# Four token tables, no arithmetic on GpSimd, a new plan: an attention, FFN and MoE kernel in FP32

## The chip, the cores and the metric

The kernel runs on one core of a Trainium2 chip. Time is the device time of one execution, in microseconds, the median of several runs. Engines: PE (TensorE), DVE (VectorE), ACT (ScalarE), POOL (GpSimd) and SP (SyncE, here a DMA queue). Each engine works through its own instructions in order.

## The reference

```python
# attention: B=4, H=12, S=448, D=64, cap=30
scores = cap * tanh(scale * q @ k.T / cap)
attn = softmax(scores)
x = (attn @ v), heads side by side       # 1792 tokens x 768
# feed-forward 768 -> 2048 -> 768
h = x @ w_in
x = (h * sigmoid(1.702 * h)) @ w_out
# top-1 mixture of 8 experts, 768 -> 1024 -> 768
e = argmax(x @ w_gate)
out = prob[e] * sigmoid(x @ w_output_gate)[e] * (relu(x @ w1[e]) @ w2[e])
```

All in FP32.

## The kernel before

**Products.** An FP32 product is made of three passes on numbers in a shorter FP32 form (fp32r): each operand is split into a high part (a cast, `rnd_any`, on ACT, DVE or POOL, lines 361, 476 and 480) and a rest (a subtraction, `rest_any`, line 484, on DVE or POOL). The passes are hi x hi, hi x lo and lo x hi. The splits of weights and of activations are most of what DVE, ACT and POOL do.

**Order.** A planner written in Python (`Plan`, from line 112) holds every piece of work as a task: its engine or a choice of engines with a cost each (`c_rnd`, `c_rest`, line 495 on), its dependencies, the buffers that it takes, a latency after it, and a due value. The due value is a place in a schedule (constants such as `W1`, `F3`, `SLOT`) less a lead by the kind of task (the table `LEAD`). The planner simulates the engines and emits each engine's instructions in the order that comes out; on the chip an engine then keeps that order, and waits for semaphores where its operands are not ready.

**Stages.** Attention runs batch by batch; per pair of heads POOL's queue carries three small transfers of the normalisation (`s_ld` L697, `s_st` L705, `r_ld` L709). The FFN runs in halves per batch (matmuls `fps`, lines 970 to 972; activation `th`, lines 990 and 994), interleaved with the attention of the batches that follow. After a batch's second half, `route` (from line 1069) works out its routing:

- `lp`, small DVE steps, and a one-hot matrix `ohb`; the matmuls `cps` (L1093 to 1096) count how many tokens of each expert come before each token;
- DVE adds the running counts `carry` and gets a position per token, `posi` (L1126 to 1130), and then the new `carry` (L1133);
- four indirect DMAs on POOL's queue (L1099), one per 112 tokens, write the token numbers to these positions of a table `tab` in DRAM. All four write the same tensor;
- the factor (probability x output gate) is written as column 768 of each token's row, and the rows go to DRAM (`x2s`).

So `route` runs four times, once per batch. After it the MoE runs in slots of 128 tokens of one expert: 20 that always run and one in a branch. The first three (`NEARLY`) take their tokens from the first three batches, the others from the counts of all four. `enumerate_tiles` (L1216 to 1238) and the three steps ahead of it (L1523 to 1525) turn the counts into slots, in some 25 small DVE steps. `token_ids` gathers the slots' rows of `tab` (POOL, `tg`, L1262), PE transposes them (`ptg`, L1269), and DVE makes token indices `gi` and output indices `si` (L1274, L1275). Per slot: gather the tokens (`xg`, POOL, L1360, ring of 3), transposes `xtp` (L1373), 36 matmuls `hps` (L1403), relu, transposes `gtp` (L1421), 48 matmuls `ops` (L1453), ACT's output scaled by column 768 of `xg` (`out_y`, L1460), and an indirect DMA to the output (POOL, L1463). A slot splits 14 chunks of weights, 6 of 1024 and 8 of 768 columns, from loads `w1r` and `w2r` into a ring of 4 (`w`) and one of 5 (`mw`) buffers.

The FFN's weights are split once, stored in DRAM (`wsp`) and loaded again (`w<-wsp`) for later batches.

Of the kernel before, what the change touches and what calls it, by code (L numbers as in the profile page):

```python
# [9 lines left out]
F32 = mybir.dt.float32  # L10
# [11 lines left out]
DM = H * D  # L22
# [19 lines left out]
LEAD = {'tanh': -0.33, 'v_hi': 0.96, 'pv2': -9.09, 'tr': 3.33, 'x2_cp': -17.4, 'relu': 1.05, 'th': 11.2, 'g_hi': 21.35, 'x2_hi': 0.71, 'x2_lo': -6.7, 'transp': 7.51, 'w_s': -0.38, 'cap_max': -2.34, 'v_lo': -4.0, 'mms': 4.58, 'x2_tr': 0.76, 'pv_x': -11.56, 'scores': 5.25, 'q_hi': -25.2, 'lo': -6.51, 'ld_qk': 12.09, 'o_acc': 2.27, 'g_lo': -9.62, 'k_hi': 5.63, 'exp': -1.51, 'p_hi': 2.76, 'eps': -23.42, 'quantum': -2.12, 'w_e': 5.66, 'st_': 3.4, 'hi': 2.08, 'gmul': -4.78, 'pv1': -8.53, 'pv_add': 1.74, 'pv_cp': 18.5, 'p_lo': 5.55, 'logit': -5.59, 'norm': -0.71, 'x_hi': 5.44, 'out_y': 2.93, 'o_x2': 5.14, 'w_1': 2.98, 'w_2': 5.49, 'x_lo': 5.68, 'recip': -20.85, 'ld': -8.2, 'ld_v': 1.8, 'k_lo': 3.19, 'q_lo': 3.16, 'u_cp': 0.0, 's_ld': 1.21, 's_rc': -0.1, 's_st': 0.07, 'r_ld': -10.16, 'f': 18.48, 'v_f': 5.49}  # L42
TICK = 10.24 / 3
WFR = 2
W1 = 117.952
W2 = 199.014
W3 = 220.117
AF1 = 0.797
AF2 = 0.777
AF3 = 0.741  # L50
AO1 = -13.626
AO2 = 7.441
AO3 = 18.073
# [8 lines left out]
ATT0 = 2.681  # L62
HID = 0
F3 = 163.508
# [9 lines left out]
SLAT = (2.8, 4.6, 5.8)
VPL = 6.822
STG = -1.173
GL = 30.335
XIN = 9.159
HL = 10.771
XAL = 41.739  # L80
SPLIT = True
CV0 = 132.598
CV1 = 66.827
MWB = 5
SLOT = 17.742
# [28 lines left out]
class Plan:  # L114
# [6 lines left out]
        ("DVE", "PE"): 0.2, ("DVE", "ACT"): 0.13, ("DVE", "DVE"): 0.13, ("DVE", "POOL"): 0.2,  # L121
# [219 lines left out]
def tile_softcap_attention_ffn_moe(  # L341
# [38 lines left out]
    tab = dram.tile([NE * ECAP, 1], F32, name="tab")  # L380
# [67 lines left out]
    def program(ctx, general):  # L448
# [82 lines left out]
        def attention(b):  # L531
# [14 lines left out]
            for h in range(H):  # L546
# [59 lines left out]
                if qkf:  # L606
                    t_q = t_k = t_qk
                else:
                    x = add({"ACT": (c_act(S, 0.19), 0.0), "POOL": (0.62, POOLD, True), "DVE": (0.36, HID, True)}, q_hi, vp, [t_qk], [qkr, qks])
# [223 lines left out]
        def single(u, c, vw):  # L833
# [32 lines left out]
            x2 = add({"POOL": (0.00083 * m + 0.16, 0.0, True), "DVE": (0.00052 * m + 0.07, HID, True)}, w_s, vw, [x], [rb, gb])  # L866
# [199 lines left out]
        routed = {}  # L1066

        def route(b, lx, lb, tcp, tokb, vq):
# [5 lines left out]
            def chain(x, eng, uses, ops):  # L1074
                for c, f in ops:
                    x = add(one(eng, c), lambda e, f=f: f(), vq, [x], uses)
                return x
# [26 lines left out]
            def lg(n):  # L1104
# [6 lines left out]
            xlt = chain(x, "DVE", [rb, tb1], [(0.13, lambda: nc.vector.tensor_copy(tl("lt", [CK, NC4, 16]), R["lp"]))])  # L1111
            xls = chain(xlt, "DVE", [rb], [
                (0.1, lambda: red(out=tl("m", [CK, NC4, 1]), in_=lg("lt"), axis=AX.X, op=ALU.max)),
                (0.1, lambda: vt(out=tl("ls", sh), in0=lg("lt"), in1=bc(R["m"], sh), op=ALU.subtract)),
            ])
            xoh = chain(xls, "DVE", [rb], [
                (0.1, lambda: vt(out=tl("eq", sh), in0=lg("lt"), in1=bc(R["m"], sh), op=ALU.is_equal)),
                (0.1, lambda: vt(out=R["eq"], in0=R["eq"], in1=bc(pr, sh), op=ALU.mult)),
                (0.1, lambda: red(out=tl("mx", [CK, NC4, 1]), in_=R["eq"], axis=AX.X, op=ALU.max)),
                (0.1, lambda: vt(out=tl("oh", sh), in0=R["eq"], in1=bc(R["mx"], sh), op=ALU.is_equal)),  # L1120
            ])
            x = chain(xoh, "DVE", [rb], [(0.1, lambda: nc.vector.tensor_copy(tl("ohb", sh, BF16), R["oh"]))])
# [475 lines left out]
```

## Time and profile before

| | before |
|---|---|
| median of 3 runs | 1177.28 us (1174.28 to 1177.40) |
| the profiled execution | 1172.92 us |
| its span | 1171.1 us |
| PE, DVE, ACT, POOL busy | 94%, 77%, 68%, 28% of the span |

The span is the stretch between the first and the last recorded instruction. Busy times are unions per engine; a matmul's end is modelled. A row of a time line gives start, duration, engine, line, operation and operands, and in brackets how long the engine stood before it and what ended that. PEclk is the granted clock of PE as a share of full speed.

### The profile page before, as it was taken

The page shows a single profiled execution, that of the slowest core. Times are in us where ns is not written, and L with a number is a line of the kernel's source. Part 1 is how long each engine was busy: PE and PEld are TensorE (multiplying, and loading weights), DVE is VectorE, ACT ScalarE, POOL GpSimd, SP SyncE. Part 2 cuts the span into 40 slices and gives each one's busy share as a digit, 9 for nine tenths or more (in the row PEclk, how much of TensorE's full clock was granted, in tenths as well). Part 3 has the DMA queues.
Part 4 walks back from the last instruction along what each step waited for, and adds up shares of the span by engine and source line. Part 5 has one row for each costly group of instructions (what it writes and reads, how often), then busy time and mean ns, then how long its engine had stood idle before and what let it go on. Part 6 is the DMA issues. An engine that isn't in the chain of part 4 may idle for free.

```text
span 1171.1 us, 16399 instructions
## 1 busy us (share of the span) xinstructions
PE 1099.8 (94%) x5378; PEld 925.9 (79%) x5378; DVE 903.7 (77%) x1467; ACT 800.7 (68%) x1302; POOL 323.0 (28%) x275
## 2 busy tenths in 40 slices
PE   5989999999989779989999999987999999999996
PEld 2446777888878668878888899865888998989986
DVE  4878899898998475686885635678998888888883
ACT  6888897777776424767783334334788888888883
POOL 0114131012211220221441101136634434344341
PEclk9999999999999979989999999998999999999999
DMA  6886668788885553643422674520159731247710
GB/s 167 226 207 189 199 193 270 233 248 245 236 268 179 99 104 106 135 134 112 119 89 84 144 107 153 225 96 21 55 189 369 290 138 47 86 157 281 264 37 26
DMA packets 70225, 191.17 MB, mean 163 GB/s; under 512 B 11362, under 2 KB 21870, under 8 KB 70128
## 3 DMA queue, kind: packets, MB, share of 16 engines
q1 hardware_dynamic: 63440, 170.62, 48.9%
q0 software_dynamic: 6464, 19.16, 5.3%
q8 instruction: 45, 0.74, 0.3%
q14 instruction: 52, 0.43, 0.2%
q10 hardware_dynamic: 224, 0.23, 0.1%
HBM read 238.82 MB, written 28.91 MB: 229 GB/s over the span
## 4 chain that ended last, share of the span: by engine, by line
PE 54%; DVE 5%; DMA 5%; issue 4%; POOL 2%; ACT 0%; SPq 0%; POOLq 0%; DVEq 0%
PE ops L1453 13%; PE hps L1403 12%; PE fps L970 7%; PE fps L971 7%; PE fps L972 7%; DMA w<-wsp 2%; DMA tab<-tokid,posi 2%; PE gtp L1421 1%; DVE mw L484 1%; POOL tab L1099 1%; PE xtp L1373 1%; PE tp L1045 1%; PE sps L637 1%; PE sps L636 1%; PE pv L664 1%
## 5 line engine op out<-in xcount | busy, mean ns | idle before, releaser
L970 PE MATMUL fps<-xh,w 128*128 128x448 f32 x384 | 146.3, 381 | 12.6 <-DVE th L994 12.6
L970 PE MATMUL fps<-gh,w 128*128 128x448 f32 x384 | 143.5, 374 | 5.1 <-DVE th L994 4.1
L971 PE MATMUL fps<-gl,w 128*128 128x448 f32 x384 | 141.8, 369 | 0.8 <-DVE gl L484 0.7
L972 PE MATMUL fps<-xh,w 128*128 128x448 f32 x384 | 141.4, 368 | 1.0 <-DVE w L484 1.0
L972 PE MATMUL fps<-gh,w 128*128 128x448 f32 x384 | 141.4, 368 | 0.8 <-POOL w L484 0.8
L971 PE MATMUL fps<-xl,w 128*128 128x448 f32 x384 | 141.8, 369 | 0.0
L645 ACT ACTIVATE p<-p,capx 112x448 f32<-112x448 f32 x192 | 126.0, 671 | 3.0
L484 DVE TENSOR_TENSOR w<-w 128x768 fp32r<-128x768 f32 (+1 forms) x80 | 86.1, 1077 | 51.7 <-ACT w L476 37.7
L641 ACT ACTIVATE p<-sps 112x448 f32<-112x448 f32 x184 | 96.6, 539 | 35.6 <-PE sps L637 29.5
L1453 PE MATMUL ops<-mw,gT 128*128 128x384 f32 x540 | 103.4, 341 | 0.0
L636 PE MATMUL sps<-qks 128*112 128x448 f32 x184 | 84.3, 458 | 15.1 <-ACT vf L476 12.4
L1403 PE MATMUL hps<-mw,xT 128*128 128x512 f32 x390 | 96.8, 402 | 0.3 <-ACT h L1416 0.3
L1453 PEld LDWEIGHTS ops<-mw,gT 128*128 128x128 f32 x540 | 94.7, 189 | 0.9
L476 ACT ACTIVATE mw<-w2r 128x768 fp32r<-128x768 f32 x89 | 74.6, 846 | 30.3 <-PE hps L1403 22.4
L476 ACT ACTIVATE w<-w 128x768 fp32r<-128x768 f32 (+1 forms) x68 | 63.0, 929 | 45.4 <-DMA w<-wsp 45.4
L970 PEld LDWEIGHTS fps<-xh,w 128*128 128x128 f32 x384 | 73.0, 190 | 26.4 <-issue 12.7
L484 DVE TENSOR_TENSOR mw<-w2r,mw 128x768 fp32r<-128x768 f32 x81 | 80.6, 1017 | 12.1 <-ACT mw L476 11.6
L1403 PE MATMUL hps<-w,xT 128*128 128x512 f32 x330 | 82.0, 398 | 8.2 <-POOL w L484 5.2
L1403 PEld LDWEIGHTS hps<-mw,xT 128*128 128x128 f32 x390 | 74.3, 191 | 17.8 <-ACT h L1416 0.6
L970 PEld LDWEIGHTS fps<-gh,w 128*128 128x128 f32 x384 | 72.8, 190 | 15.9 <-DVE th L994 4.5
L1453 PE MATMUL ops<-w,gT 128*128 128x384 f32 x420 | 82.0, 343 | 1.0 <-ACT y L1460 1.0
L484 DVE TENSOR_TENSOR hl<-p,hl 112x448 fp32r<-112x448 f32 x105 | 69.1, 660 | 16.0 <-ACT hl L476 15.6
(240 smaller groups left out, 2537.9 us busy)
## 6 DMA issues: line engine op xcount, KB each, us to landing
w1r<-in_w_dram SPq DMA_DIRECT2D x60, 1024.0 KB
w2r<-in_w_dram SPq DMA_DIRECT2D x80, 768.0 KB
w<-wsp SPq DMA_DIRECT2D x56, 384.0 KB
w<-wsp SPq DMA_DIRECT2D x42, 512.0 KB
qkr<-in_qk_dram SPq DMA_DIRECT2D x95, 224.0 KB
wr<-in_w_in_dram SPq DMA_DIRECT2D x32, 384.0 KB
wr<-in_w_out_dram SPq DMA_DIRECT2D x24, 512.0 KB
x2s<-x2tok SPq DMA_DIRECT2D x4, 1358.0 KB
```

What stands on the lines that cost most here:

```text
L476: nc.scalar.activation(o, i, AF.Copy)
L484: e.tensor_tensor(out=o, in0=x, in1=f32(hi), op=ALU.subtract)
L636: mm(sps, lhsT=t[:, 1, sl], rhs=t[:, 0, :], start=True, stop=False)
L637: mm(sps, lhsT=t[:, 2, sl], rhs=t[:, 0, :], start=False, stop=True)
L641: nc.scalar.activation(p, T["s", kc], AF.Tanh, scale=sct2[:CK] if qkf else 1.0)
L645: nc.scalar.activation(p, p, AF.Exp, scale=capx[:CK])
L664: mm(o, lhsT=VSh[:, 0, c, :], rhs=t[:, 0, :], start=c == 0, stop=False)
L970: mm(fps, lhsT=wh, rhs=xh, start=c == 0, stop=False)
L971: mm(fps, lhsT=wh, rhs=xl, start=False, stop=False)
L972: mm(fps, lhsT=wl, rhs=xh, start=False, stop=c == n - 1)
L1403: mm(T["h", s][n], lhsT=x_[:, kk, :], rhs=w[:, a, n * 512:(n + 1) * 512], start=st_, stop=sp_)
L1453: mm(T["o", s][:, n, :384], lhsT=x_[:, k, :], rhs=w[:, a, n * 384:(n + 1) * 384], start=st_, stop=sp_)
```

## The change

- **Tables.** `tab` becomes a list of four tensors, one per 112 tokens of a batch (`tab[j]`). Each scatter of a route writes its own. The four are cleared by four transfers, due later than the one before. `token_ids` gathers from all four (`tq`, L1266) and a DVE reduction adds them (`one_table`, L1273).
- **POOL.** `c_rnd`, `c_rest`, `q_hi` and `w_s` lose POOL as a choice, so casts are on ACT or DVE and rests on DVE alone. POOL keeps its DMAs and the set-up of constants.
- **The plan.** The four scatters of a route no longer depend on each other, and the enumeration depends on the counts (`counted[b]`, the last `carry`), not on scatters. Small DVE steps cost 0.22 instead of 0.1 or 0.12 and take the lock on the port. The gather of a slot counts 10.0 us of POOL with a latency of 3 instead of 1.04 with 8 (`GATH`). All numbers of `LEAD` and most constants are other ones; the diff shows some.
- **Factor.** ACT copies column 768 of `xg` to a small tile `fc` (ring of 4, L1382) near the slot's transposes; `out_y` reads `fc`, and `xg` is free after the transposes. Its ring goes from 3 to 2.

```diff
-W1 = 117.952
+W1 = 123.44
-F3 = 163.508
+F3 = 157.954
+GATH = 10.0
-SLOT = 17.742
+SLOT = 17.899
...
-    tab = dram.tile([NE * ECAP, 1], F32, name="tab")
+    tab = [dram.tile([NE * ECAP, 1], F32, name=f"tab{j}") for j in range(NC4)]
...
         def c_rnd(n):
-            return {"ACT": (c_act(n), 0.0), "POOL": (0.00083 * n + 0.16, POOLD, True), "DVE": (0.00052 * n + 0.07, HID, True)}
+            return {"ACT": (c_act(n), 0.0), "DVE": (0.00052 * n + 0.07, HID, True)}
 
         def c_rest(n):
-            return {"DVE": (c_dve(n), 0.0, True), "POOL": (0.0021 * n + 0.16, RESTD, True)}
+            return one("DVE", c_dve(n), True)
...
-                    out=tab[:, :], out_offset=bass.IndirectOffsetOnAxis(ap=R["posi"][:, j:j + 1], axis=0),
+                    out=tab[j][:, :], out_offset=bass.IndirectOffsetOnAxis(ap=R["posi"][:, j:j + 1], axis=0),
...
-            for j in range(NC4):
-                x = add(one("POOL", 1.04), lambda e, j=j: scatter(j), vq, [x], [rb], lat=2.0)
-            routed[b] = [x, prev_carry[0]]
+            routed[b] = [add(one("POOL", 1.04), lambda e, j=j: scatter(j), vq, [x], [rb], lat=6.0) for j in range(NC4)]
+            counted[b] = prev_carry[0]
+            routed[b].append(prev_carry[0])
...
-        add(one("SP", 0.3), lambda e: nc.sync.dma_start(tab.rearrange("(p a) b -> p (a b)", p=128), zer), WGV)
+        for t in tab:
+            add(one("SP", 0.5), lambda e, t=t: nc.sync.dma_start(t.rearrange("(p a) b -> p (a b)", p=128), zer), 60.0)
...
-        mg = ms.enter_context(tc.tile_pool(name="mg", bufs=3, reuse_waits="tile"))
+        mg = ms.enter_context(tc.tile_pool(name="mg", bufs=2, reuse_waits="tile"))
...
-            def gather_ids(e):
+            def gather_ids(j):
+                if j == 0:
+                    mt(f"tq{g}", [n, NC4, TS])
                 nc.gpsimd.indirect_dma_start(
-                    out=mt(f"tg{g}", [n, TS]), out_offset=None, in_=tab.rearrange("(a b) c -> a (b c)", b=TS),
+                    out=M[f"tq{g}"][:, j, :], out_offset=None, in_=tab[j].rearrange("(a b) c -> a (b c)", b=TS),
                     in_offset=bass.IndirectOffsetOnAxis(ap=M[f"tri{g}"][:, 0:1], axis=0),
                 )
+
+            def one_table(e):
+
+                red(out=last(mt(f"tg{g}", [n, TS])), in_=M[f"tq{g}"].rearrange("n j t -> n t j"), axis=AX.X, op=ALU.add)
...
+            def factor_in(e):
+                T["fc", s] = mx.tile([128, 1], F32, tag="fc", name="fc", bufs=4)
+                nc.scalar.activation(T["fc", s], T["xg", s][:, DM:DM + 1], AF.Copy)
...
-                nc.scalar.activation(T["y", s], T["o", s][:, :, :384], AF.Copy, scale=T["xg", s][:, DM:DM + 1])
+                nc.scalar.activation(T["y", s], T["o", s][:, :, :384], AF.Copy, scale=T["fc", s])
...
-        x = steps(routed[B - 2], v, [
+        x = steps(counted[B - 2], v, [
...
-        x = steps([early] + routed[B - 1], v, [
+        x = steps([early, counted[B - 1]], v, [
```

**POOL's order around the first route, before.** `sm`, `rs` and `r` are the normalisation of a pair of heads; the rows at L484 and L361 are rests and casts.

```order
L697 DMA sm<-u 128x1x7
L484 TENSOR_TENSOR w<-w 128x768
L1099 DMA tab<-tokid,posi 14336x1
L705 DMA rs<-sm 128x7
L1099 DMA tab<-tokid,posi 14336x1 x2
L361 TENSOR_SCALAR w<-w 128x768
L1099 DMA tab<-tokid,posi 14336x1
L484 TENSOR_TENSOR qks<-qkr,qks 128x448
L484 TENSOR_TENSOR vs<-vr,vs 112x4x64
L709 DMA r<-rs 64x896
```

The same place in the changed kernel (lines are one higher there):

```order
L698 DMA sm<-u 128x1x7
L706 DMA rs<-sm 128x7
L1100 DMA tab_68<-tokid,posi 14336x1
L1100 DMA tab_69<-tokid,posi 14336x1
L1100 DMA tab_70<-tokid,posi 14336x1
L1100 DMA tab_71<-tokid,posi 14336x1
L710 DMA r<-rs 64x896
L698 DMA sm<-u 128x1x7
```

The scatters stand together, each on its own table, and the cast of `w` that stood between the third and the fourth is not on POOL any more.

**DVE's order behind the last route's counts, before.** `nt` is the first step of the enumeration.

```order
L1133 TENSOR_TENSOR carry<-cps,carry 128x8
L480 CAST w<-w1r_7331 128x1024
L484 TENSOR_TENSOR mw<-w1r_7331,mw 128x1024
L484 TENSOR_TENSOR w<-w1r_7331,w 128x1024
L484 TENSOR_TENSOR mw<-w2r_7398,mw 128x768
L367 TENSOR_TENSOR gT<-gtp,gT 128x512
L367 TENSOR_TENSOR xT<-xtp,xT 128x512
L484 TENSOR_TENSOR mw<-w2r_7429,mw 128x768
L484 TENSOR_TENSOR mw<-w2r_7808,mw 128x768 x2
L480 CAST w<-w1r_7366 128x1024
L480 CAST w<-w2r_7398 128x768
L484 TENSOR_TENSOR w<-w1r_7366,w 128x1024
```

After three further rows `nt` comes. The same place in the changed kernel:

```order
L1134 TENSOR_TENSOR carry<-cps,carry 128x8
L1542 TENSOR_TENSOR nt__7143<-carry,t_133 128x112
L1543 TENSOR_REDUCE te<-nt__7143 128x8
L1544 TENSOR_TENSOR te<-te,tk 128x8
L1218 TENSOR_TENSOR le<-eid 128x64
```

The enumeration follows the counts at once, 28 rows in a piece, and the rests that stood ahead of it stand behind it.

**DVE's order behind that enumeration in the changed kernel**, its second half, up to the reduction of the four gathered parts (`tg<-tq`) and the indices `gi`, for which the slots' gathers wait.

```order
L485 TENSOR_TENSOR w<-w2r_7341,w 128x768
L368 TENSOR_TENSOR gT<-gtp,gT 128x512
L485 TENSOR_TENSOR mw<-w2r_7341,mw 128x768
L485 TENSOR_TENSOR mw<-w2r_7379,mw 128x768
L368 TENSOR_TENSOR xT<-xtp,xT 128x256
L485 TENSOR_TENSOR mw<-w2r_7379,mw 128x768
L485 TENSOR_TENSOR mw<-w2r_7804,mw 128x768
L1273 TENSOR_REDUCE tg_8091<-tq_8015 18x128
L485 TENSOR_TENSOR mw<-w2r_7804,mw 128x768
L1285 CAST gi_8106<-ptg 128x18
```

Ten rests and four subtractions of turned activations stand between the enumeration and the reduction; before, `gi` stood behind a cast, two rests and two such subtractions, without a reduction.

## Rows read from the trace of the kernel before

**Rows 1.** The page, parts 1, 4 and 5.

```profile
PE 1099.8 (94%) x5378; PEld 925.9 (79%) x5378; DVE 903.7 (77%) x1467; ACT 800.7 (68%) x1302; POOL 323.0 (28%) x275
...
PE ops L1453 13%; PE hps L1403 12%; PE fps L970 7%; PE fps L971 7%; PE fps L972 7%; DMA w<-wsp 2%; DMA tab<-tokid,posi 2%; PE gtp L1421 1%; DVE mw L484 1%; POOL tab L1099 1%; PE xtp L1373 1%; PE tp L1045 1%; PE sps L637 1%; PE sps L636 1%; PE pv L664 1%
...
L476 ACT ACTIVATE w<-w 128x768 fp32r<-128x768 f32 (+1 forms) x68 | 63.0, 929 | 45.4 <-DMA w<-wsp 45.4
```

**Rows 2.** Waits of PE: engine, line <- releaser: us in total, times, longest us.

```profile
PE fps L970 <- DVE th L994: 16.7, 5, 10.4
...
PE hps L1403 <- POOL w L484: 5.2, 1, 5.2
PE cps L1094 <- DVE ohb L1122: 5.0, 3, 3.5
...
PE hps L1403 <- DVE w L480: 2.6, 1, 2.6
```

**Rows 3.** Stretches: us, busy PE, PEld, DVE, ACT, POOL, PEclk, DMA share, GB/s.

```profile
100.00:300.00 200.00, 196.96 (x919) 161.50 (x918) 179.06 (x334) 157.97 (x299) 39.28 (x44) 1.00 0.77 228
300.00:340.00 40.00, 36.46 (x177) 30.46 (x175) 38.90 (x65) 31.68 (x58) 7.12 (x8) 1.00 0.86 254
...
400.00:420.00 20.00, 9.61 (x42) 8.16 (x41) 9.06 (x14) 4.62 (x7) 3.98 (x4) 0.74 0.40 40
420.00:440.00 20.00, 15.91 (x67) 13.89 (x66) 13.60 (x20) 5.31 (x8) 6.57 (x6) 0.83 0.43 119
440.00:460.00 20.00, 20.00 (x109) 17.82 (x108) 13.72 (x22) 9.47 (x16) 2.60 (x4) 1.00 0.40 121
...
500.00:520.00 20.00, 16.92 (x68) 13.64 (x67) 17.95 (x27) 11.39 (x21) 6.74 (x10) 0.83 0.51 138
520.00:540.00 20.00, 20.00 (x99) 17.15 (x99) 15.18 (x28) 15.76 (x28) 1.98 (x4) 1.00 0.50 141
...
880.00:1140.00 260.00, 260.00 (x1388) 235.30 (x1388) 219.29 (x243) 218.44 (x284) 101.84 (x58) 1.00 0.50 185
```

**Rows 4.** Time line of POOL, first route: start, duration, instruction, [idle before].

```profile
384.25 2.28 POOL L484 TENSOR_TENSOR w<-w 128x768 fp32r<-128x768 f32 x1 [3.48 <-DVE ps__4231 L1127]
387.30 1.02 POOL L1099 DMA_INDIRECT tab<-tokid,posi  x1 [0.76 <-DVE sm L701]
...
408.02 0.84 POOL L361 TENSOR_SCALAR w<-w 128x768 fp32r<-128x768 f32 x1
414.47 1.02 POOL L1099 DMA_INDIRECT tab<-tokid,posi  x1 [5.61 <-DMA tab<-tokid,posi]
```

**Rows 5.** Time line of DVE, first route.

```profile
408.89 0.96 DVE L484 TENSOR_TENSOR w<-w 128x768 fp32r<-128x768 f32 x1 [13.35 <-POOL w L361]
```

**Rows 6.** Time line of DVE, second route.

```profile
500.27 2.04 DVE L484 TENSOR_TENSOR vs<-vr,vs 112x256 fp32r<-112x256 f32 x1 [5.35 <-POOL vs L361]
```

**Rows 7.** Time line of POOL, last route.

```profile
789.44 4.37 POOL L1099 DMA_INDIRECT tab<-tokid,posi  x1 [5.43 <-DVE carry L1133]
```

**Rows 8.** Time line of DVE, last route.

```profile
789.14 0.68 DVE L480 CAST w<-w1r 128x1024 fp32r<-128x1024 f32 x1
...
804.72 0.26 DVE L1523 TENSOR_TENSOR nt__7137<-carry,t 128x112 f32<-128x112 f32 x1
...
807.87 6.41 DVE L1224 TENSOR_SCALAR es<-es 128x18 f32<-128x18 f32 x1
```

**Rows 9.** DMA issues: out<-in, xcount, median us to landing.

```profile
tab<-tokid,posi POOLq DMA_INDIRECT x16, 7.9
```

**Rows 10.** DVE by form, 880 to 1140 us: busy, mean ns, idle before.

```profile
L484 DVE TENSOR_TENSOR mw<-w1r,mw 128x1024 fp32r<-128x1024 f32 x40 | 46.6, 1221 | 0.3
```

**Rows 11.** Time line of DVE in a slot.

```profile
979.75 0.69 DVE L480 CAST w<-w1r 128x1024 fp32r<-128x1024 f32 x1
...
982.75 3.49 DVE L484 TENSOR_TENSOR mw<-w1r,mw 128x1024 fp32r<-128x1024 f32 x3
986.15 0.69 DVE L367 TENSOR_TENSOR xT<-xtp,xT 128x512 fp32r<-128x512 f32 x1
```

More of the change, by code (lines that the diff above doesn't have):

```diff
@@ L73 @@
 WEB = 2
[L74 to L80, printed above, removed]
+SLAT = (4.2, 4.6, 5.8)
+VPL = 1.869
+STG = -3.554
+GL = 37.536
+XIN = 11.584
+HL = 10.021
+XAL = 79.95
 SPLIT = True
-CV0 = 132.598
-CV1 = 66.827
+CV0 = 129.09
+CV1 = 54.183
 MWB = 5
-SLOT = 17.742
+SLOT = 17.899
 MLEAD = 0.0
@@ L120 @@
         ("ACT", "PE"): 0.28, ("ACT", "ACT"): 0.05, ("ACT", "DVE"): 0.15, ("ACT", "POOL"): 0.18,
-        ("DVE", "PE"): 0.2, ("DVE", "ACT"): 0.13, ("DVE", "DVE"): 0.13, ("DVE", "POOL"): 0.2,
+        ("DVE", "PE"): 0.2, ("DVE", "ACT"): 0.13, ("DVE", "DVE"): 0.0, ("DVE", "POOL"): 0.2,
         ("POOL", "PE"): 0.14, ("POOL", "ACT"): 0.15, ("POOL", "DVE"): 0.15,
@@ L608, in attention @@
                 else:
-                    x = add({"ACT": (c_act(S, 0.19), 0.0), "POOL": (0.62, POOLD, True), "DVE": (0.36, HID, True)}, q_hi, vp, [t_qk], [qkr, qks])
+                    x = add({"ACT": (c_act(S, 0.19), 0.0), "DVE": (0.36, HID, True)}, q_hi, vp, [t_qk], [qkr, qks])
                     t_q = add(one("DVE", c_dve(S) + 0.06, True), q_lo, vp, [x], [qkr, qks])
@@ L865, in single @@
             x1 = add(one("ACT", c_act(m)), w_e, vw, [x], [rb, eb])
-            x2 = add({"POOL": (0.00083 * m + 0.16, 0.0, True), "DVE": (0.00052 * m + 0.07, HID, True)}, w_s, vw, [x], [rb, gb])
+            x2 = add(one("DVE", 0.00052 * m + 0.07, True), w_s, vw, [x], [rb, gb])
             return add(one("DVE", c_dve(m), True), w_1, vw, [x1, x2], [eb, gb]), rb, eb
@@ L1075, in chain @@
                 for c, f in ops:
-                    x = add(one(eng, c), lambda e, f=f: f(), vq, [x], uses)
+                    x = add(one(eng, c, eng == "DVE"), lambda e, f=f: f(), vq, [x], uses)
                 return x
@@ L1207, in steps @@
             for f in ops:
-                x = add(one("DVE", 0.12), lambda e, f=f: f(), v, [x] if not isinstance(x, list) else x)
+                x = add(one("DVE", 0.22, True), lambda e, f=f: f(), v, [x] if not isinstance(x, list) else x)
             return x
@@ L1271, in token_ids @@
             y = steps(x, v, [lambda: vt(out=mt(f"inv{g}", [128, n]), in0=bc(rid, [128, n]), in1=M[f"lim{g}"], op=ALU.is_ge)])
-            x = add(one("POOL", 1.04), gather_ids, v, [x], lat=3.0)
+            xs = []
+            for j in range(NC4):
+                xs.append(add(one("POOL", 1.04), lambda e, j=j: gather_ids(j), v, [x] + xs[-1:] + routed[B - 2 if g == 0 else B - 1], lat=3.0 if j == NC4 - 1 else 0.0))
+            x = add(one("DVE", 0.7, True), one_table, v, xs)
             x = add(one("PE", 0.1), turn, v, [x], [tb])
@@ L1363, in gather @@
                 )
-            x = xg_[s] = add(one("POOL", 1.04), gather, v - SLOT, [ids[g][0]] + routed[B - 2 if g == 0 else B - 1], [xgb[s]], lat=8.0)
+            x = xg_[s] = add(one("POOL", GATH), gather, v - SLOT, [ids[g][0]] + routed[B - 2 if g == 0 else B - 1], [xgb[s]], lat=3.0)
+            fcb[s] = r_fc.new()
+            def factor_in(e):
+                T["fc", s] = mx.tile([128, 1], F32, tag="fc", name="fc", bufs=4)
+                nc.scalar.activation(T["fc", s], T["xg", s][:, DM:DM + 1], AF.Copy)
+            fin[s] = add(one("ACT", 0.2), factor_in, v - XIN, [x], [xgb[s], fcb[s]])
             done = []
@@ L1466, in scatter_y @@
                 )
-            x = add(one("ACT", c_act(768, 0.15)), out_y, v + 8, [x], [ob, yb, xgb[s]])
+            x = add(one("ACT", c_act(768, 0.15)), out_y, v + 8, [x, fin[s]], [ob, yb, fcb[s]])
             add(one("POOL", 1.04), scatter_y, v + 8, [x, ids[g][1]], [yb], lat=3.0)
```

75 lines of the change are left out of this document (38 added, 37 removed).

## The prediction

> **What bounds the kernel now.** I read the page first. PE is busy for 1099.8 of 1171.1 us, 94% of the span, DVE for 77% and POOL for 28%, and the chain that ended last is PE for more than half, but it also holds "DMA tab<-tokid,posi" with 2%: the scatters into the table stand on the path [rows 1]. So PE is the bound except where something late holds it, and the question is where. The waits of PE answer that: the two largest waits in the middle are the first matmul of a product on DVE's th, 16.7 us in five waits with one of 10.4, and, at the last route, waits on DVE's ohb, DVE's w and POOL's w [rows 2]. Each wait also lowers the granted clock, so that the idle time alone understates it. I therefore read PE's loss off the stretches. From 400 to 440 us PE ran 42 and 67 matmuls, at granted clocks of 0.74 and 0.83; the 20 us behind it hold 109 at 1.00. Forty microseconds did the work of twenty: **20 us lost at the first route**. From 500 to 520 it ran 68 where the next 20 us hold 99: 20 x (1 - 68/99) = **6.3 us lost at the second**. From 880 to 1140 PE is busy for all of 260 us at 1.00: in the slots nothing is to be had unless PE's own work shrinks, and it does not [rows 3].
>
> The engines' own time lines say why. At the first route POOL issues its four scatters between 387.30 and 414.47 us; each waits until the one before has landed, since all write one tensor. The third has POOL's cast of a weight chunk behind it, which therefore runs only at 408.02 [rows 4]. DVE stands from 395.54 to 408.89, 13.35 us, for that cast, and behind it in DVE's order stands the th that PE wants [rows 5]. At the second route it is the same: DVE stands 5.35 us for POOL's cast of vs, which stands behind the fourth scatter [rows 6]. At the last route the counts (carry) are complete when the first scatter starts, at 789.44 [rows 7], but the enumeration of the slots starts on DVE at 804.72, because the plan lets it wait for the scatters; one of its steps of 18 elements takes 6.41 us, beside POOL's rests [rows 8].
>
> **The change, part by part.** The sum is against the profiled execution, 1172.92 us, which is 4.36 below the median of the three runs, 1177.28.
>
> *Four tables, no arithmetic on POOL: first and second route.* POOL's order now has the four scatters in a row, then normalisation transfers, and no cast or rest anywhere. Four issues of about 1.02 us [rows 4] take 4 us instead of the 27.2 us from 387.30 to 414.47, and DVE has nothing left to wait for on POOL. What is late next is r<-rs, whose chain of three transfers now stands behind 4 us of scatters, and the w loads: ACT waits 45.4 us in all for w<-wsp [rows 1]. So not all of the 20 us comes back. Of PE's 16.7 us on th, 6.3 lie in four waits other than the long one [rows 2]; I put half of them down to this supply and keep 3 us: **-17**, ends 0 and -20. At the second route, keeping 2: **-4.3**, ends 0 and -6.3. The third route lost under 2 us: 0.
>
> *The last route.* PE's waits there are 3.5 on ohb, 2.6 on DVE's w and 5.2 on POOL's w [rows 2], with two small ones 12.0 us. In the new order the enumeration follows carry at once. Its 20-odd steps at about 0.3 us come to some 6.8 us, in which DVE does no rest. PE has some 4 us of products ready then, so it stands about 3.5 us. The gathers of the four tables start when the enumeration is done, 8 us after cps. The last scatter, issued some 5 us after cps, lands 7.9 us later by the median [rows 9], at 13; its gather and the reduction of the four parts follow, and the reduction stands behind ten rests on DVE, at about 20. PE reaches ptg after 13.5 us of products and 3.5 us of wait, so it stands another 3 to 4 us. The wait for ohb shrinks, because DVE's rest ahead of it no longer runs beside POOL. Together 7 us instead of 12: **-5**, ends +3 (all of today's waits stay and the reduction adds 3) and -10.
>
> *POOL's arithmetic goes to DVE and ACT ahead of the first route.* A rest of 128x768 takes 2.28 us on POOL [rows 4] and 0.96 on DVE [rows 5], a factor of 0.42. From 100 to 300 us POOL is busy for 39.28 us, so DVE gets at most 16.5 on top of its 179.06, 196 of 200 us; from 300 to 340 it gets 3.0 on top of 38.90, 41.9 of 40 [rows 3]. The first fits, the second does not, by 1.9 us. I take **+3**: 1.9 and one for waits in order elsewhere. Ends: 0, since DVE's instructions also lose the neighbour that stretched them, and +8.5 (19.5 us moved, less half of the 22.0 us in which DVE stands idle in those 240 us).
>
> *The slots.* A slot lasts 18.35 us of PE, and has 14 rests. DVE does 12 of them now and is busy for 219.29 of 260 us, 15.5 per slot; it takes two more rests and a cast. At the mean of a rest of 1024 columns, 1.22 [rows 10], 0.96 for one of 768 [rows 5] and 0.69 for the cast [rows 11] that is 18.4. But rests that run back to back, with nothing on POOL beside them, start every 1.13 us (three from 982.75 to 986.15) [rows 11], 0.09 below the mean; with that off each of the 14, DVE needs 17.1. I take 17.1, since POOL's arithmetic is what stretches the mean, and it is gone. PE stays the bound and the term is **0**; the other end is a rival below. ACT, busy for 218.44 of 260 us [rows 3], has 2.9 us of slack per slot for the copies of the factor column, which are one element wide.
>
> *At nothing.* The four clears of 57 KB are 1 us of transfer at 228 GB/s [rows 3], in a stretch in which SP's loads run ahead; without that cover 1 us. The ring of two for xg: the factor copy frees a buffer at the transposes instead of at the output, and a gather has most of a slot of 18.35 us to land. The other three gathers of table parts are in the last-route term.
>
> Sum: -17 - 4.3 - 5 + 3 = -23.3, so 1149.6 on the profiled execution's scale, and with 4.4 for the median **1154.0 us**.
>
> One row speaks against the change. The scatter at 789.44 took 4.37 us, where the usual one takes 1.02; DVE had begun a cast of 1024 columns just before, at 789.14, and went on with rests [rows 4, 7, 8]. The Trainium skill ("SBUF — State Buffer", section "SBUF: two separate sides") says that DMAs issued from GpSimd are starved while VectorE runs instructions of a two-port mode, such as a cast of fp32, since GpSimd cannot write their descriptors then. By that rule the busier DVE would stretch the POOL issues. By the rows it happened to one scatter of four there, and the sum goes without it; it is the fourth rival.
>
> **Rivals.**
> 1. *More comes back.* With POOL gone from the shared work every DVE instruction runs at its own pace; all of 20 + 6.3 returns, the last route keeps 2 us instead of 7, and the +3 becomes 0. That is -36.3: 1141, and a little lower if PE's 3 us of idle time from 100 to 300 go too. For it: the 6.41 us of a tiny step [rows 8]. Against it: DVE is nearly full ahead of the first route. It decides if DVE stays under 95% from 100 to 340.
> 2. *The wait is only replaced.* PE's product waits for th behind w<-wsp loads or normalisation in the stretch from 390 to 440, and half of the first two losses stay: -13.2 - 2 + 3 = -12: 1165. For it: ACT's 45.4 us on w<-wsp [rows 1].
> 3. *DVE becomes the bound in the slots*: slower. If DVE needs 17.1 us per slot and the 2.9 us of idle time that it has per slot today (it waits there for ACT's halves) stay, a slot lasts 20.0, 1.6 more, and 17 slots cost 27: 1181. The turn lies at 1.25 us of idle per slot. For it: the mean of a rest, 1.22 us [rows 10]. Against: nine weight buffers between DVE and PE, and DVE's waits today come because it is ahead.
> 4. *POOL's issues starve.* Eight scatters and gathers at the last route at 3.35 us more each are 27 us, of which I let 14 reach PE: 1168. The Trainium skill's page named above gives the mechanism.
> 5. *The scatters wait on each other all the same*, through something else than the tensor. Then the chain of 27 us stays, without casts behind it: 1170 to 1177.
>
> **How the numbers follow.** My forecast, 1142 to 1166, has 0.58; the first rival 0.14, the second 0.10, the third 0.12, the fourth 0.04, the fifth 0.02. About 0.3%, 3.5 us, is what a measurement can tell from no change. The ends of the terms without the slots, taken together, give 1141 (all the gains) to beyond 1177. The range from 1134 to 1178 holds the forecast, the second, fourth and fifth rivals, most of the first and some of the third. Faster: 0.56 of the forecast, all of the first, 0.08 of the second, 0.06 of the rest, 0.84. Same: 0.07, from the edges of the second, fourth and fifth. Slower: 0.09, the third and a little of the fifth.
>
> **What would show it.** Right: POOL's scatters at the first route stand about 1 us apart; no DVE wait on POOL is left; PE's wait for th falls from 16.7 us to under 5; the granted clock from 400 to 440 is near 1.00; the enumeration starts right after carry; PE's busy share from 880 to 1140 stays at 100%, with DVE at 93 to 95%. Wrong: idle time of PE in the slots that DVE releases; POOL issues of 4 us and more at the last route; more than 8 us of idle PE time from 100 to 340.

## The result, and the profile after

The changed kernel takes 1144.33 us, the median of four runs (1141.25 to 1148.28), against 1175.78 us of the kernel before on the same chip: a ratio of 0.9737, with a 95% interval from 0.9694 to 0.9779. That is 31.5 us less. Forecast were 1154.0, in a range from 1134 to 1178. The profiled execution took 1141.25 us, the fastest of the four, with a span of 1139.5.

Engines in the page of the changed kernel, part 1, beside [rows 1]: PE is busy for 9.7 us less (its mean granted clock is 0.992 of full speed, where it was 0.982); DVE for 30 us more; POOL for 113 us less.

```profile
PE 1090.1 (96%) x5378; PEld 918.4 (81%) x5378; DVE 933.4 (82%) x1606; ACT 779.3 (68%) x1308; POOL 209.7 (18%) x158
```

The waits of PE in the changed kernel (in total, times, longest), beside [rows 2]. One on ACT's vf, 12.1 us in the first 100 us, is left out; it was 12.4 before.

```profile
...
PE fps L971 <- ACT w L477: 8.2, 2, 6.7
PE sps L637 <- ACT p L642: 8.2, 10, 2.5
PE gtp L1440 <- ACT h L1435: 4.1, 1, 4.1
PE ptg L1277 <- DVE tg L1273: 2.7, 2, 1.6
...
PE fps L971 <- DVE th L995: 0.7, 2, 0.4
```

The 16.7 us on DVE's th are 0.7, and no wait of PE on POOL is left. In their place stands one wait of 6.7 us on ACT's half of a weight chunk, at the first route. Stretches of the changed kernel (columns as in [rows 3]):

```profile
100.00:300.00 200.00, 194.81 (x908) 157.85 (x907) 185.31 (x362) 165.45 (x327) 15.66 (x26) 1.00 0.76 223
300.00:340.00 40.00, 38.71 (x187) 32.73 (x186) 39.29 (x72) 35.55 (x67) 1.63 (x3) 1.00 0.82 266
...
400.00:420.00 20.00, 16.02 (x71) 14.25 (x72) 13.57 (x22) 11.23 (x17) 1.17 (x2) 0.83 0.41 105
420.00:440.00 20.00, 20.00 (x107) 17.78 (x106) 17.58 (x30) 8.95 (x16) 1.85 (x3) 1.00 0.43 115
...
850.00:1110.00 260.00, 260.00 (x1396) 235.32 (x1395) 246.32 (x287) 208.59 (x283) 101.95 (x27) 1.00 0.50 183
```

At the first route PE stands once, from 397 to 404 us, and the stretch from 400 to 420 is short of matmuls, 71 where the next has 107. In the slots PE is still busy all the time, with DVE at 246.32 of 260 us, 95%.

To see where the 32 us came from I count for each stretch what PE lost: its length, less each matmul at its start-to-start distance at full clock (0.205 us for 448 columns, 0.233 for 512, 0.176 for 384, about 0.1 for a transpose of 128). The stretches are cut at each kernel's own routes (the matmuls `lp`), so that they hold like work; the last column holds the last route and the slots. "To 100" holds work on inputs as they arrive and the last column leaves out what comes after the last matmuls; both are to be compared between kernels only. Differences under 2 us, or 3 in the last column, tell nothing, since the distances per matmul are not known better.

| PE's loss, us | to 100 | 100 to 1st route | 1st route | 2nd | 3rd | last route, slots |
|---|---|---|---|---|---|---|
| before | 48.2 | 18.2 | 19.7 | 8.1 | 5.4 | 16.5 |
| the change | 42.7 | 17.6 | 9.0 | 4.2 | 5.3 | 4.2 |
| four tables alone | 43.7 | 24.3 | 11.9 | 3.3 | 9.5 | 21.9 |
| no POOL arithmetic alone | 45.0 | 21.1 | 14.7 | 2.7 | 3.2 | 18.3 |
| both | 47.0 | 20.8 | 2.5 | 3.3 | 11.9 | 26.1 |
| both, enumeration behind the counts | 46.8 | 20.5 | 3.0 | 5.6 | 10.5 | 25.5 |
| the change with the old numbers | 48.2 | 28.0 | 5.3 | 7.2 | 9.7 | 8.9 |
| the change, one table | 42.7 | 17.9 | 21.8 | 0.3 | 5.9 | 21.3 |
| the change, POOL arithmetic back | 44.6 | 28.5 | 16.9 | 15.1 | 9.7 | 11.7 |

A route's column holds the stretch up to the next route as well; the expectations below count some 50 us from each route on, which gives 8.7, 4.1 and 3.7 for the change. Each row is one profiled execution; a column moves by some us where the plan orders the work anew, and from one execution to the next as well: in four kernels below whose order of work is that of the change (without the scatters of batch 0, rows of 784, the store from ACT's queue, the store ahead of the scatters) the first route's column reads 10.9, 14.3, 10.9 and 8.2. The last seven rows are experiments.

### The profile page after: what moved, and what is told of

Same layout as the page of the kernel before. It is cut to its first block, busy times and chain, and to the rows that moved or that the text cites. A ratio compares the mean times of both kernels' runs of the same rounds, so it can differ in the third digit from the quotient of the medians.

```text
span 1139.5 us, 16349 instructions
## 1 busy us (share of the span) xinstructions
PE 1090.1 (96%) x5378; PEld 918.4 (81%) x5378; DVE 933.4 (82%) x1606; ACT 779.3 (68%) x1308; POOL 209.7 (18%) x158
## 5 line engine op out<-in xcount | busy, mean ns | idle before, releaser
L1482 POOL DMA_INDIRECT out_dram<-y,si x20 | 109.8, 5491 | 179.8 <-ACT y L1479 171.2
L485 DVE TENSOR_TENSOR w<-w 128x768 fp32r<-128x768 f32 (+1 forms) x98 | 104.1, 1068 | 42.7 <-ACT w L477 42.3
L642 ACT ACTIVATE p<-sps 112x448 f32<-112x448 f32 x184 | 97.2, 543 | 32.0 <-PE sps L638 17.4
L637 PE MATMUL sps<-qks 128*112 128x448 f32 x184 | 80.5, 437 | 21.5 <-ACT vf L477 12.1
L477 ACT ACTIVATE w<-w 128x768 fp32r<-128x768 f32 (+1 forms) x78 | 71.8, 924 | 31.1 <-DMA w<-wsp 31.1
L477 ACT ACTIVATE mw<-w2r 128x768 fp32r<-128x768 f32 x79 | 67.0, 848 | 33.9 <-PE hps L1422 29.1
L485 DVE TENSOR_TENSOR mw<-w1r,mw 128x1024 fp32r<-128x1024 f32 x65 | 77.1, 1220 | 5.6 <-ACT mw L477 5.6
```

The lines of the kernel that those rows point to most:

```text
L477: nc.scalar.activation(o, i, AF.Copy)
L485: e.tensor_tensor(out=o, in0=x, in1=f32(hi), op=ALU.subtract)
L637: mm(sps, lhsT=t[:, 1, sl], rhs=t[:, 0, :], start=True, stop=False)
L642: nc.scalar.activation(p, T["s", kc], AF.Tanh, scale=sct2[:CK] if qkf else 1.0)
L1482: nc.gpsimd.indirect_dma_start(out=out[:, :], out_offset=bass.IndirectOffsetOnAxis(ap=M[f"si{g}"][:, i:i + 1], axis=0), in_=T["y", s].rear ...
```

## The experiments

A measured figure is the time as a ratio to the kernel before, run on the same chip, with its 95% interval; us are worked out from it.

**Four tables alone**, in the kernel before.

```diff
-    tab = dram.tile([NE * ECAP, 1], F32, name="tab")
+    tab = [dram.tile([NE * ECAP, 1], F32, name=f"tab{j}") for j in range(NC4)]
...
-            for j in range(NC4):
-                x = add(one("POOL", 1.04), lambda e, j=j: scatter(j), vq, [x], [rb], lat=2.0)
+            routed[b] = [add(one("POOL", 1.04), lambda e, j=j: scatter(j), vq, [x], [rb], lat=6.0) for j in range(NC4)]
```

> The kernel before with four tables and nothing else of the change: scatters no longer wait on each other, POOL keeps its casts and rests, the plan keeps its numbers, and the enumeration still waits for the scatters in the plan. (The gathered parts of the two groups of slots share their memory, so that the ring of three still fits.) Theory A, the chain of scatters with arithmetic behind it makes the stalls of the first two routes: both mostly go, -10.6 and -2.6 us as measured in the changed kernel, and 2 us at the last route; about 1160. Theory B, the new numbers of the plan bring the gain, and the structure little: 1170 to 1178. Theory C, what counts is that POOL does no arithmetic: the casts still stand behind four issues and beside DVE, so 1165 to 1175, with DVE's waits on POOL's cast still there.

Measured: 0.9968 (0.9940 to 0.9996). The first route's loss went from 19.7 to 11.9 and the second's from 8.1 to 3.3, as theory A has it, and 4.5 went in the first 100 us, but 6.1 came between 100 us and the first route, 4.1 at the third and 5.4 at the last. The scatters were on the path, and the end of their chain is worth 3 to 4 us to the whole. The time, 1174.37 us, lies in the ranges of theories B and C and not in that of A; of C's reason nothing is seen, since DVE's wait on POOL's cast is not what remained.

**No arithmetic on POOL alone**, in the kernel before.

```diff
-            return {"DVE": (c_dve(n), 0.0, True), "POOL": (0.0021 * n + 0.16, RESTD, True)}
+            return one("DVE", c_dve(n), True)
```

and the same in `c_rnd`, `q_hi` and `w_s`.

> The kernel before without POOL as a choice for casts and rests, and nothing else of the change; the scatters stay chained. Theory A says that the chain alone does no harm where no cast stands behind it: the first two routes gain 13 us, the stretch ahead of the first route 6 us as in the changed kernel, the last route a few for the neighbour gone: about 1152. Theory B: 1170 to 1178. Theory C: 1150 or below, nearly all of the gain.

Measured: 0.9837 (0.9775 to 0.9900), some 19 us, between the theories. The chain of scatters alone is not harmless: 14.7 us are still lost at the first route, where 2.5 are with four tables added (below).

**One table in the changed kernel.**

```diff
-                    out=tab[j][:, :], out_offset=bass.IndirectOffsetOnAxis(ap=R["posi"][:, j:j + 1], axis=0),
+                    out=tab[0][:, :], out_offset=bass.IndirectOffsetOnAxis(ap=R["posi"][:, j:j + 1], axis=0),
```

> The changed kernel, in which all scatters write the first of the four tables (the others stay zero, the sum is the same), so that they wait on each other again; order and plan are untouched. Theory A: nothing but normalisation transfers stands behind the chain at the first two routes, so they lose 0 to 8 us; at the last route the gather waits for a last scatter that lands some 25 us later than now, and PE stands 10 to 15 us for ptg: 1155 to 1168. Theory C: only the last route loses, 1154 to 1158. If chained scatters cost nothing anywhere: 1144.

Measured: 0.9872 (0.9824 to 0.9919) against 0.9737, so about 16 us slower than the changed kernel; theory A's 1155 to 1168 holds. Waits of PE in this kernel:

```profile
PE ptg L1277 <- DVE tg L1273: 16.5, 2, 15.0
...
PE tp L1046 <- DVE x L1026: 11.2, 3, 9.9
```

The first is the last route: ptg waits for the reduction, that for the gathers, and those for a fourth scatter that goes out 18.7 us after the first, instead of 4:

```profile
776.97 0.96 POOL L1100 DMA_INDIRECT tab<-tokid,posi  x1 [22.41 <-DVE carry L1134]
...
795.64 0.93 POOL L1100 DMA_INDIRECT tab<-tokid,posi  x1 [4.34 <-DMA tab<-tokid,posi]
```

The second is the first route: the normalisation transfer r<-rs stands in POOL's queue behind the fourth scatter and goes out at 421.74. Here one edit changes nothing but the waits, since the order is the same. So four tables are worth 16 us in this kernel, and 4 in the one before.

**POOL's arithmetic back in the changed kernel.**

```diff
-            return one("DVE", c_dve(n), True)
+            return {"DVE": (c_dve(n), 0.0, True), "POOL": (0.0021 * n + 0.16, RESTD, True)}
```

and the same in `c_rnd`, `q_hi` and `w_s`, with the old `RESTD` and `POOLD`.

> The changed kernel with POOL back as a choice for casts and rests, at the costs of the kernel before; tables, enumeration and numbers of the plan stay. Theory A: the first two routes stay as they are now, the 6 us ahead of the first route are lost again and some 5 us at the last route, where small steps stand beside POOL's rests: 1150 to 1158. Theory C: 1165 or more. Theory B: within 4 us of 1144.

Measured: 1.0093 (1.0068 to 1.0118), 42 us slower than the changed kernel and slower than the one before. Theory A falls here: I had let the first two routes stay as they are, and they lose 16.9 and 15.1 us instead of 9.0 and 4.2, though the scatters stand together, with 0.3 us between them. Only theory C's "1165 or more" holds the time. Waits of PE from 380 to 700 us:

```profile
PE sps L637 <- ACT p L642: 11.3, 2, 11.1
PE fps L971 <- DVE th L995: 6.4, 2, 3.9
PE tp L1046 <- DVE x L1026: 6.4, 2, 4.6
```

**Both parts on the kernel before**, with its plan, without and with the enumeration's tasks behind the counts.

```diff
-        x = steps([early] + routed[B - 1], v, [
+        x = steps([early, counted[B - 1]], v, [
```

> The kernel before with two parts of the change: four tables, and no arithmetic on POOL (plan numbers, costs of small steps, enumeration behind the scatters, ring of three stay). Alone the tables gave 3 us and the other 16. Theory D, now held: each part alone removes the stalls of the first two routes, but leaves a price that the other one removes (with POOL's arithmetic the tables' gathers and DVE stand beside it at the start of the slots; with one table the slots' gathers wait for the chain). Together they then give more than 3 + 16: 1148 to 1155. If the parts simply add or overlap: 1158 to 1164. If the new numbers of the plan are what makes them work together: 1160 or more.

> The same, with the enumeration's tasks behind the counts alone in the plan and not behind the scatters. Theory D: the gathers of the token numbers come some 10 us earlier at the last route, worth 0 to 5 us there, nothing elsewhere: 1145 to 1153. If the enumeration was never what the slots waited for: the same as without it.

Measured: 1.0019 (0.9990 to 1.0048) and 0.9937 (0.9910 to 0.9965). Theory D falls as a whole: together the parts give nothing, less than the second alone. The expectation that the parts need the new numbers, 1160 or more, holds for the first kernel's 1173.16 us. The enumeration behind the counts gives some 0.8%, with intervals that lie apart, so the slots did wait for it. The two rows of the table don't show this, since the profiled execution was one of the faster for the first kernel (1168.74 us) and the slowest of six for the second (1170.70, median 1165.70).

Theory D's first half stands: at the first route 2.5 us are left of 19.7. But in the last column, at the start of the slots above all, 26.1 us are lost. POOL's time line there, of the kernel without the counts:

```profile
814.72 10.16 POOL L1370 DMA_INDIRECT xg<-x2s,gi  x1 [2.01 <-DVE si L1285]
825.18 0.96 POOL L1370 DMA_INDIRECT xg<-x2s,gi  x1 [0.30 <-issue]
...
849.91 7.95 POOL L1370 DMA_INDIRECT xg<-x2s,gi  x1 [0.30 <-issue]
```

PE at that place, a wait and a row of its time line:

```profile
PE ops L1463 <- DVE mw L484: 7.4, 1, 7.4
...
827.82 1.12 PE L1383 MATMUL xtp<-ident,xg 128*128 128x128 f32 x4 [4.48 <-DMA xg<-x2s,gi]
```

The issue of a gather takes 10.16 us instead of 0.96, and PE stands 4.48 us for its data; before that it stood 7.4 us for a rest on DVE. DVE at that place works from 813.15 without a break:

```profile
816.19 0.67 DVE L480 CAST w<-w1r 128x1024 fp32r<-128x1024 f32 x1
816.79 4.61 DVE L484 TENSOR_TENSOR w<-w1r,w 128x1024 fp32r<-128x1024 f32 x4
821.33 2.68 DVE L484 TENSOR_TENSOR mw<-w2r,mw 128x768 fp32r<-128x768 f32 x3
829.60 0.69 DVE L367 TENSOR_TENSOR xT<-xtp,xT 128x512 fp32r<-128x512 f32 x1 [5.59 <-ACT xT L476]
```

It ends at 824.0, and the issue at 824.9. In the kernel with the counts the same gather takes 10.62 us, and there PE's one long wait, 14.2 us, is for it:

```profile
814.97 10.62 POOL L1371 DMA_INDIRECT xg<-x2s,gi  x1 [1.53 <-DVE si L1286]
...
PE xtp L1384 <- DMA xg<-x2s,gi: 18.9, 4, 14.2
```

This is the starving of POOL's issues that the prediction had as its fourth rival, mostly in another place: not at the tables, but at the tokens of the first slots.

**The changed kernel with the old numbers** (`LEAD` and the constants; `GATH` as in the change).

```diff
-W1 = 123.44
+W1 = 117.952
...
-SLOT = 17.899
+SLOT = 17.742
```

> The changed kernel with the table of leads and the constants of the kernel before (GATH as in the change): what the new numbers are worth by themselves. Theory D: the structure carries the gain, and this stays within 8 us of the changed kernel, 1144 to 1152. Theory B, the numbers carry it: 1160 or more.

Measured: 0.9944 (0.9922 to 0.9966). Theory B's range holds: all of the structure on the old numbers gives 6 to 7 us, and **the numbers, put on this structure, give the other 2.1%, about 24 us**. By the table, 15.9 of them are ahead of the first route (48.2 + 28.0 against 42.7 + 17.6), 3.0 at the second, 4.4 at the third and 4.7 behind; at the first route they cost 3.7. Waits of PE up to 385 us, with the old numbers,

```profile
PE sps L637 <- DVE qks L595: 8.4, 8, 3.5
PE fps L973 <- DVE w L485: 6.7, 3, 3.3
PE sps L637 <- ACT p L642: 4.7, 7, 2.0
```

and with the new ones:

```profile
PE sps L637 <- ACT p L642: 5.7, 9, 1.6
PE sps L637 <- DVE qks L595: 1.0, 1, 1.0
```

With the old numbers PE waits for 15.1 us on two kinds of rest that DVE makes late, those of w, which POOL shared before, and those of q (L595), which were DVE's already; in the kernel before these waits were under 3 us. But the new numbers don't stand by themselves either: with POOL's arithmetic back the kernel that has them, the tables and the rest of the change loses 0.9% on the kernel before. So they look fitted to this division of the work; the new numbers on the kernel before were not run, and which of them count was not tried.

**The gather counted as short again.**

```diff
-GATH = 10.0
+GATH = 1.04
```

and its latency 8 instead of 3.

> The changed kernel with the gather of a slot's tokens counted as before in the plan, 1.04 us of POOL and a latency of 8, instead of 10 and 3. In the two kernels with four tables and no POOL arithmetic on the old plan, PE stood 10 to 19 us for gathers at the start of the slots, and the changed kernel does not at all. Theory G, the long gather in the plan spaces the gathers of the first slots behind the last route and so removes this wait: undone, PE waits on xg again and the slots lose 8 to 20 us: 1152 to 1165. Rival, the other parts (early factor, costs of small steps, new numbers) removed it: 1142 to 1147.

Measured: 0.9742 (0.9707 to 0.9777), no difference from the changed kernel's 0.9737. PE does not wait for a gather. Theory G falls for the changed kernel. What took the 17 us of the last column away lies in the structure that the kernel with the old numbers has too (8.9 us): the ring, the early factor, the costs of small steps, or the long gather on the old numbers, where it was not undone. Those were not tried one by one. Undoing the early factor with a ring of two was not tried either.

**Without the scatters of batch 0.**

```diff
             def scatter(j):
+                if b == 0:
+                    return
```

> The changed kernel without the four scatters of the first batch; everything else and its order stay. The token numbers of the first batch are left out of the tables. It asks what held the loads of weights at the first route, where PE still stands 6.7 us: from 388 to 394 and from 398 to 402 the DMA engines moved 11 to 147 GB/s with loads outstanding, each time behind packets of the scatters. Theory S, the scatters hold the DMA engines: the wait goes, PE loses 2 us at the first route instead of 8.7, and the time is 1136 to 1140. Rival, the store of 1.36 MB that is issued in the same stretch is in front of them: the wait stays, 1143 to 1146.

Measured: 0.9715 (0.9686 to 0.9745). The kernel leaves out the token numbers of batch 0, so its output is not that of the others. At the first route the wait stayed, 8.0 us, which I first took as the end of theory S. I had named the wrong route: the halves of batch 1 come before the second half of batch 0, so that batch 0 is routed second. Stretches at the second route, of the changed kernel,

```profile
468.00:472.00 4.00, 4.00 (x21) 3.66 (x20) 3.69 (x8) 3.02 (x5) 0.00 (x0) 1.00 1.05 45
472.00:476.00 4.00, 4.00 (x21) 3.42 (x21) 0.88 (x2) 2.87 (x5) 0.00 (x0) 1.00 0.48 30
476.00:480.00 4.00, 4.00 (x21) 3.20 (x19) 0.26 (x1) 0.00 (x0) 0.00 (x0) 1.00 0.76 88
480.00:484.00 4.00, 1.50 (x5) 1.21 (x5) 3.90 (x7) 2.90 (x5) 0.00 (x0) 0.78 1.04 335
```

and without these scatters:

```profile
468.00:472.00 4.00, 4.00 (x21) 3.65 (x20) 3.29 (x7) 3.03 (x6) 0.00 (x0) 1.00 0.43 135
472.00:476.00 4.00, 4.00 (x21) 3.48 (x21) 3.88 (x6) 3.47 (x6) 0.00 (x0) 1.00 0.57 178
476.00:480.00 4.00, 4.00 (x22) 3.34 (x21) 3.86 (x8) 3.29 (x7) 0.00 (x0) 1.00 0.37 127
480.00:484.00 4.00, 4.00 (x21) 3.49 (x20) 3.97 (x7) 3.39 (x8) 0.00 (x0) 1.00 0.52 158
```

The last columns are the ones to read: with the scatters the DMA engines move 30 to 88 GB/s for 12 us and then 335, and PE stands; without, 127 to 178 all along, PE loses nothing, and the second route's loss goes from 4.2 to 0.3 us. So theory S holds there, for these 4 us. In the whole it can't be told from the changed kernel, since the intervals overlap; other places lost as much in the profiled execution (7.6 instead of 4.2 us at the last route).

**Rows of 784 elements, and the store from ACT's queue.** Both came from the wrong reading just told: I looked for the cause in the store of the rows that goes out beside the scatters.

```diff
-ROWW = 776
+ROWW = 784
```

> The changed kernel with token rows of 784 elements (3136 bytes, a multiple of 64) instead of 776 (3104 bytes, none); order and plan are the same. The scatters are not what slows the loads at the routes: without those of the first batch the wait on a load of weights stayed (8.0 us), and the DMA engines were slow in the same places. What is common to the three slow stretches is the store of 448 rows just before and in them. Theory R, the odd row length makes the writes slow, and they hold the loads behind them: PE's losses at the first three routes (8.7, 4.1 and 3.7 us) halve or better, 1134 to 1139. Rival, any store of this size does: no change, 1142 to 1146.

```diff
-            routed[b].append(add(c, lambda e: nc.sync.dma_start(x2s[b * S:(b + 1) * S, :].rearrange("(j p) w -> p j w", p=CK), T["tok", b]),
+            routed[b].append(add(c, lambda e: nc.scalar.dma_start(x2s[b * S:(b + 1) * S, :].rearrange("(j p) w -> p j w", p=CK), T["tok", b]),
```

> The changed kernel with the same store issued from ACT's queue instead of SP's, so that the loads of weights do not stand behind it in one queue; order and plan are otherwise the same. Theory Q, the loads wait in the queue behind the store: PE's losses at the first three routes halve, 1134 to 1139. Rival, the writes slow the memory or the DMA engines whatever the queue: no change, 1142 to 1147.

Measured: 0.9764 (0.9725 to 0.9803) and 0.9752 (0.9717 to 0.9787). Neither differs from the changed kernel, so the two rivals ("no change") hold.

**The store ahead of the first scatter**, at three routes.

```diff
                 vt(out=t[:, :, DM:DM + 1], in0=R["so"], in1=R["sm"], op=ALU.mult)
+                if b < B - 1:
+                    places()
+                    for j in late:
+                        scatter(j)
```

`places` makes posi, and `late` holds the scatters that the plan emitted ahead of it.

> The changed kernel in which, at the first three routes, DVE makes the positions (posi) right behind the factor column instead of ahead of it, 3 to 5 steps later; the order of every engine is otherwise the same. So the store of the rows is issued before the first scatter and not 1 us behind it. The reading so far: the batch whose scatters were left out earlier is routed second (the halves of batch 1 come first), and it is at the second route that the slow stretch went and PE's loss fell from 4.1 to 0.0 us; each burst of scatter packets slows the DMA engines for 6 to 10 us, and at the first route of the changed kernel the packets leave in two bursts, at 385 (the first scatter) and 395 (the other three), where at the second they leave together behind the store. If the two bursts are what PE's wait of 6.7 us at the first route comes from, one burst behind the store leaves 0 to 3 us of it: 1137 to 1142. Rival, the slow stretches sum up to the same however they lie: within 2 us of the changed kernel.

Measured: 0.9710 (0.9686 to 0.9734) and 1142.47 us, 0.5 above the expected range and within the rival's 2 us of the changed kernel. The interval overlaps the changed kernel's, so that it is no faster by this measurement. At the first route the packets leave in one burst, and PE's wait there is 4.6 instead of 6.7 us, where 0 to 3 were expected; the route's column reads 8.2 instead of 9.0, which is no difference. The slow stretch is one instead of two (a wait of PE, then two stretches):

```profile
PE fps L971 <- DVE th L995: 6.8, 3, 4.6
...
392.00:396.00 4.00, 4.00 (x21) 3.66 (x21) 2.51 (x4) 1.28 (x2) 0.00 (x0) 1.00 0.88 41
396.00:400.00 4.00, 3.96 (x20) 3.30 (x18) 0.00 (x0) 0.00 (x0) 0.00 (x0) 1.00 0.64 32
```

That the slow stretches sum up to much the same however they lie, the rival, is not refuted.

Nothing that was run is clearly faster than the changed kernel.

## Why the prediction was right, and where not

The time lies in the range and on the right side, 9.7 us below the forecast. That the sum came so near is in good part luck: two terms that were far off, the structure and the numbers, made up for each other. By its own steps:

- **First route, -17.** The mechanism was right: the scatters stand together and DVE waits for nothing on POOL. With tables and no POOL arithmetic on the old plan the loss falls by 17.2 us, the forecast term; in the change it falls by 10.7 in the profiled execution. The sign that I had named, a granted clock near 1.00 from 400 to 440, holds from 420 on only (0.83 and 1.00). The rest stands behind what the prediction named as late next, the loads of w. POOL's scatters go out at once in the changed kernel,

```profile
383.30 1.02 POOL L1100 DMA_INDIRECT tab<-tokid,posi  x1 [38.59 <-DVE carry L1134]
384.62 2.65 POOL L1100 DMA_INDIRECT tab<-tokid,posi  x1 [0.30 <-issue]
...
388.81 1.52 POOL L1100 DMA_INDIRECT tab<-tokid,posi  x1 [0.30 <-issue]
```

  and ACT waits for a load:

```profile
403.08 1.58 ACT L477 ACTIVATE w<-w 128x768 fp32r<-128x768 f32 x2 [8.86 <-DMA w<-wsp]
```

  The load lies in slow stretches behind two bursts of scatter packets, with 39 GB/s behind the first, 262 between them and 118 behind the second, while PE stands (columns as in [rows 3]):

```profile
388.00:392.00 4.00, 4.00 (x21) 3.68 (x20) 2.85 (x6) 0.54 (x1) 2.03 (x2) 1.00 0.77 39
392.00:396.00 4.00, 4.00 (x22) 3.66 (x21) 1.92 (x4) 0.54 (x1) 0.00 (x0) 1.00 0.76 262
...
400.00:404.00 4.00, 0.02 (x1) 0.03 (x1) 0.04 (x1) 0.92 (x2) 0.00 (x0) 0.54 0.82 118
```

  That a burst makes them slow is shown at the second route alone; at the first it is argued, since leaving these scatters out was not tried. I had costed the scatters as POOL issues and not as DMA traffic.
- **Second route, -4.3.** 3.9 measured. **Third, 0.** No difference (5.4 and 5.3).
- **Last route, -5.** -12.3 measured, with the slots. The step that failed is the size: I took PE's idle time, 12.0 us, though I had said that idle time understates a loss, and read only the first two routes off the stretches. These are the stretches of the kernel before that I should have read:

```profile
780.00:800.00 20.00, 15.84 (x77) 12.06 (x75) 17.30 (x32) 7.85 (x12) 10.70 (x5) 0.91 0.45 166
800.00:820.00 20.00, 12.12 (x51) 10.80 (x52) 19.42 (x35) 8.31 (x12) 12.22 (x8) 0.83 0.01 1
```

  The granted clock was 0.91 and 0.83 there, and the last column has 16.5 us of loss. What stays is less than I thought, too: 4.1 us for ACT's h and 1.1 for ptg.
- **Ahead of the first route, +3.** It went to -6.1. By itself the structure costs 9.8 us there (old numbers), a little beyond my upper end of 8.5; the new numbers give back 15.9. I had costed the numbers at nothing, without saying so. This is the step that failed most, and it hid itself: the structure on the old numbers is worth 6 to 7 us and not 23, and the numbers on the new structure 24 and not 0. The two are not to be added in another order: without the division of work the numbers gain nothing, as the run with POOL's arithmetic shows.
- **Slots, 0.** Right: DVE is busy for 17.4 us of 18.35 per slot (I had 17.1), and PE for all of them. The third rival did not come.
- **The row against the change.** POOL's output scatters in the slots take 6.07 us to issue,

```profile
L1482 POOL DMA_INDIRECT out_dram<-y,si x15 | 91.1, 6070 | 141.9 <-ACT y L1479 141.9
```

  where before they took 1.57:

```profile
L1463 POOL DMA_INDIRECT out_dram<-y,si x15 | 23.5, 1565 | 3.8 <-ACT mw L476 1.7 <-issue 1.1
```

  PE waits for no output, so it costs nothing here; the gathers of the slots take 1.00. On the old plan a gather took 10.16 and 10.62, and PE stood 4.5 and 14.2 us for it. So the fourth rival's mechanism is there, and the places decide. The Trainium skill ("SBUF — State Buffer", section "SBUF: two separate sides") says that DMAs issued from GpSimd are starved of descriptors while VectorE runs an instruction of a two-port mode, for which it names the fp32 copy. The traces agree that the issue is long where DVE works without a break, but not on the instruction: beside the 10.16 us DVE ran two casts and otherwise subtractions with two inputs, and beside the output scatters in the slots subtractions alone. Here the measurement decides. One slot of the changed kernel, POOL and then DVE:

```profile
886.60 6.05 POOL L1482 DMA_INDIRECT out_dram<-y,si  x1 [9.22 <-ACT y L1479]
...
886.46 2.70 DVE L485 TENSOR_TENSOR mw<-w2r,mw 128x768 fp32r<-128x768 f32 x3
889.07 3.79 DVE L485 TENSOR_TENSOR w<-w2r,w 128x768 fp32r<-128x768 f32 x4
```

## What to carry to other kernels

Price a stall by the work done in its stretch against a full one, everywhere and not only where it is large: idle time leaves out the slower clock around it (here 12.0 us of idle time stood for 16.5 of loss). A change that comes with a new set of schedule numbers is two changes; price both, or say that one is not priced. And when work leaves an engine that also issues DMAs, look at what then runs beside those issues, and give the time to the one that somebody waits for.

## What the runs showed of the hardware

A burst of four scatters of 112 elements of 4 bytes slowed the DMA traffic of the core far beyond its size: at the second route 30 to 88 GB/s for some 12 us where 127 to 178 flowed without it, with loads of up to 512 KB outstanding. And an indirect DMA's issue on POOL, about 1 us where nothing holds it, took 10.16 and 10.62 us beside a DVE that worked without a break, ending 0.9 us after DVE's run, and 6.07 on average in the slots of the changed kernel, where DVE was busy for 95% of the time with subtractions beside these issues. That DVE's subtractions hold the issue is read from these coincidences; no run changed them alone.
